# Idle matmuls at the head of a fused attention and feed-forward kernel: 116 tiny ones on four row groups and 11 wide ones, in place of 78 narrow ones

## The chip, the cores and the metric

One core of one Trainium2 chip. The metric is the time of one execution in device microseconds. One early run of the kernel before took 371.03 us and is left out throughout.

## The reference, cut to what matters

```python
# attention inside chunks of 64 tokens: q, k, v are (8, 8, 576, 64)
scores = scale * np.matmul(q_c, k_c.transpose(0, 1, 2, 4, 3))
scores = scores - np.max(scores, axis=-1, keepdims=True)
attn = np.exp(scores)
attn = attn / (np.sum(attn, axis=-1, keepdims=True) + 1e-09)
out = np.matmul(attn, v_c)
# then a feed-forward block on 4608 tokens of 512: w_in is (512, 2048), w_out is (2048, 512)
h = x @ w_in
g = h * (1.0 / (1.0 + np.exp(-beta * h)))
return (g @ w_out)
```

The two big products make up most of the work. The attention of the first tokens has to be done before the first big product can start, so the first 25 us are a chain of small steps.

## The kernel before: the parts that matter here

```python
    def emit_idle(n, w):                       # products of zeros; nobody reads the result
        d = ps_p.tile([128, 512], FP32, tag="p", name="warm")
        for _ in range(n):
            nc.tensor.matmul(out=d[:, 0:w], lhsT=idle[:, 0:128], rhs=idle[:, 0:w])
    ...
        nc.vector.memset(idle, 0.0)
        nc.vector.memset(braw, 0.0)
        ...                                    # loads of q, k, v and the weights are issued here
        emit_idle(78, 128)                     # TensorE has nothing else to do yet
        emit_T_half(0)                         # DVE transposes of the first half of q and k
        emit_sc_half(0, 0)                     # 32 score matmuls: the first group
        emit_ex_half(0, 0)
        emit_idle(4, 512)
        emit_T_half(1)
        emit_sc_half(0, 1)                     # 96 score matmuls in these three: the second group
        emit_ex_half(0, 1)
        emit_sc_half(1, 0)
        emit_sc_half(1, 1)
        emit_ex_half(1, 0, 2)
        ...
        emit_pv(0, ("s", "p"))                 # value matmuls, 32 and 32
        emit_norm(0, 0)                        # DVE: reciprocal and product
        emit_norm(0, 1)
        emit_pv(1, ("x", "p"))
        ...
        emit_xt_pe(0, 0)                       # transposes on TensorE, copies on ACT
        emit_xt_pe(0, 1)
        a0, v0 = emit_m(0, 0, 0, 256, True)    # the first big product starts here
        a1, v1 = emit_m(0, 1, 0, 256, True)
```

Each matmul is two instructions, a weight load and the product (the page of before counts 2754 of each). "Own instruction n" below is the n-th of these in program order.

The softmax here doesn't subtract the row's maximum and nothing guards it: scores larger than these inputs give would overflow.

## Time and profile before

| | before |
|---|---|
| median, lowest of the first runs | 295.28, 294.66 us |
| span of the profiled run | 294.1 us |
| first score group starts | 8.32 us |
| second score group starts | 10.17 us |
| TensorE stops in the value matmuls | 11.62 to 14.94 us |
| first big product starts | 18.40 us |
| half clock | 14.87 to 21.70 us |

Times inside a run count from the span's start. The prediction quotes the lines for most of this. In a timeline line the columns are start, length, engine, source line, operation, tiles, shapes and count, and in brackets the idle time just before and what ended it; "issue" there means that the profile shows nothing that was waited for. PE is a product of TensorE and PEld its weight load; DVE is VectorE, ACT ScalarE and POOL GpSimd. "Half clock" is a granted TensorE clock of 0.5.

### The profile page before, as it was taken

How to read it: one execution, taken by the hardware profiler on the slowest of the kernel's cores; microseconds unless marked ns; L12 is line 12 of the kernel's file. 1: busy time of each engine (PE TensorE's matmuls, PEld its weight loads, DVE VectorE, ACT ScalarE, POOL GpSimd, SP SyncE). 2: the span in 40 equal slices, each digit the busy share in tenths (PEclk: the TensorE clock that was granted, in tenths of full speed). 3: DMA queues.
4: the chain of work that ended last, by engine and by line, in shares of the span. 5: the costliest groups of instructions: out<-in, count | busy, mean ns of one | idle time of the engine just before them, and what ended most of it. 6: DMA issues, size and time to landing. Idle time of an engine off the chain costs nothing.

```text
span 294.1 us, 6595 instructions
## 1 busy us (share of the span) xinstructions
PE 281.8 (96%) x2754; PEld 139.8 (48%) x2754; DVE 140.5 (48%) x250; ACT 147.4 (50%) x225; POOL 95.6 (33%) x124
## 2 busy tenths in 40 slices
PE   8389999999999999999999899999999999999996
PEld 8255445545544444444444444444444444444444
DVE  2367813687455845453545253635363536444300
ACT  4338615785446655445544555545555554544411
POOL 8753768607624796070807060000000000000000
PEclk9959999999999999999999999999999999999999
DMA  8999999999979999999999999242525212101012
GB/s 197 177 197 207 181 175 169 245 108 94 174 98 136 177 178 153 175 159 170 105 187 104 184 116 173 74 107 50 130 72 109 44 63 71 42 36 38 36 71 71
DMA packets 139996, 37.13 MB, mean 126 GB/s; under 512 B 126912, under 2 KB 135488, under 8 KB 139968
## 3 DMA queue, kind: packets, MB, share of 16 engines
q0 software_dynamic: 99136, 17.83, 81.2%
q1 hardware_dynamic: 40688, 18.83, 29.4%
q8 instruction: 21, 0.34, 0.5%
q10 hardware_dynamic: 144, 0.07, 0.1%
q14 instruction: 7, 0.06, 0.1%
HBM read 36.71 MB, written 9.44 MB: 157 GB/s over the span
## 4 chain that ended last, share of the span: by engine, by line
PE 91%; ACT 2%; issue 2%; DVE 2%; DMA 2%; SPq 0%; DVEq 0%
PE hps L310 43%; PE ops L342 41%; PE x L262 2%; DMA raw<-in_k_dram 2%; PE sc L234 1%; PE sc L221 1%; PE ops L543 1%; ACT xt L295 1%; DVE t L175 1%; PE xp L294 1%; DVE x L278 1%; ACT osb L352 0%; ACT h L174 0%; ACT et L204 0%; PE sc L194 0%
## 5 line engine op out<-in xcount | busy, mean ns | idle before, releaser
L324 DVE SCALAR_TENSOR_TENSOR gt<-sg,hps 128x512 f16<-128x512 f32 (+1 forms) x152 | 99.3, 658 | 116.6 <-ACT sg L320 116.4
L310 PE MATMUL hps<-xt,win 128*128 128x512 f16 (+1 forms) x608 | 138.0, 371 | 2.2 <-ACT xt L295 1.2
L320 ACT ACTIVATE sg<-hps,beta 128x512 f32<-128x512 f32 (+1 forms) x152 | 100.4, 665 | 76.0 <-PE hps L310 76.0
L342 PE MATMUL ops<-wout,gt 128*128 128x512 f16 x560 | 131.3, 379 | 0.0
L310 PEld LDWEIGHTS <-win 128*128 128x128 f16 x608 | 58.3, 99 | 64.2 <-issue 3.2
L342 PEld LDWEIGHTS <-gt 128*128 128x128 f16 x560 | 53.7, 98 | 63.1
L352 ACT ACTIVATE osb<-ops 128x512 f32<-128x512 f32 x35 | 20.9, 598 | 42.2 <-PE ops L342 42.2
L110 POOL DMA_DIRECT2D vbig<-in_v_dram x40 | 34.1, 873 | 8.2 <-DMA wout<-in_moe_w_out_dram 3.7
L96 POOL DMA_DIRECT2D qu<-in_q_dram x22 | 18.7, 862 | 45.2 <-DMA qT<-qu 35.2
L278 DVE TENSOR_TENSOR x<-x,rd 128x512 f16<-128x512 f32 x34 | 23.5, 691 | 1.3
L96 POOL DMA_DIRECT2D ku<-in_k_dram x22 | 18.8, 879 | 0.0
L276 DVE RECIPROCAL rd<-x 128x8 f32<-128x8 f32 x34 | 6.8, 201 | 15.4 <-PE x L262 15.4
L262 PE MATMUL x<-vbig,et 64*64 64x65 f16 x544 | 8.1, 196 | 3.5 <-issue 3.3
L262 PEld LDWEIGHTS <-et 64*64 64x64 f16 x576 | 6.4, 111 | 10.1 <-issue 6.4
L243 ACT ACTIVATE et<-sc 128x1024 f16<-128x1024 f32 (+1 forms) x8 | 6.4, 811 | 8.5 <-PE sc L234 8.5
L295 ACT COPY xt<-xp 128x512 f16<-128x512 f16 x12 | 6.7, 588 | 7.6 <-PE xp L294 7.6
L227 ACT ACTIVATE et<-sc 128x1024 f16<-128x1024 f32 x10 | 10.2, 1015 | 0.0
L359 PE MATMUL warm<-idle 128*128 128x128 f16 (+1 forms) x82 | 7.2, 264 | 1.2 <-DVE braw L363 1.2
L102 POOL DMA_DIRECT2D ku<-in_k_dram x9 | 6.8, 752 | 3.4 <-DMA win<-in_moe_w_in_dram 1.5
L102 POOL DMA_DIRECT2D qu<-in_q_dram x9 | 6.8, 761 | 2.5 <-DMA win<-in_moe_w_in_dram 1.3
L359 PEld LDWEIGHTS <-idle 128*128 128x128 f16 x82 | 6.3, 119 | 1.5 <-DVE braw L363 1.2
L555 DVE TENSOR_SCALAR osb<-ops 128x256 f32<-128x256 f32 (+1 forms) x2 | 0.7, 358 | 12.1 <-PE ops L543 12.1
(36 smaller groups left out, 68.8 us busy)
## 6 DMA issues: line engine op xcount, KB each, us to landing
out_dram<-osb SPq DMA_DIRECT2D x35, 256.0 KB, 3.6
vbig<-in_v_dram POOLq DMA_DIRECT2D x32, 128.0 KB, 7.0
qu<-in_q_dram POOLq DMA_DIRECT2D x20, 128.0 KB, 5.0
ku<-in_k_dram POOLq DMA_DIRECT2D x20, 128.0 KB, 6.2
win<-in_moe_w_in_dram POOLq DMA_DIRECT2D x8, 256.0 KB, 9.3
wout<-in_moe_w_out_dram POOLq DMA_DIRECT2D x4, 512.0 KB, 12.1
qu<-in_q_dram POOLq DMA_DIRECT2D x3, 256.0 KB, 7.2
ku<-in_k_dram POOLq DMA_DIRECT2D x3, 256.0 KB, 7.7
```

What stands on the lines that cost most here:

```text
L96: nc.gpsimd.dma_start(out=tv[off:off + n, sp], in_=src[b, :, s:s + n, :].rearrange("h p d -> p h d"),)
L102: nc.gpsimd.dma_start(out=t[off // 2:(off + n) // 2], in_=src[b, :, s:s + n, :].rearrange("h (p r) d -> p h r d", r=2),)
L110: nc.gpsimd.dma_start(out=vbig[off:off + n, i, :, 0:D], in_=v[b, :, s:s + n, :].rearrange("h p d -> p h d"),)
L227: nc.scalar.activation(out=et, in_=sc, func=ACTF.Exp, scale=scale)
L262: nc.tensor.matmul(out=(x[0][64 * c:64 * c + 64, r, g, 0:D + 1] if len(x) == 1 else x[r][64 * c:64 * c + 64, g, 0:D + 1]), lhsT=(et[64 * r ...
L278: nc.vector.tensor_tensor(out=o, in0=z[..., 0:D], in1=rd[:, r].to_broadcast(list(o.shape)), op=ALU.mult)
L310: nc.tensor.matmul(out=hps[:, 0:n], lhsT=w_in16[m // 2][:, kk, (m % 2) * 128:(m % 2) * 128 + 128], rhs=xr[:, c0 // CH:(c0 + n) // CH, 2 * ...
L320: nc.scalar.activation(out=sg[:, 0:n], in_=hps[:, 0:n], func=ACTF.Tanh, scale=beta2[:, m:m + 1])
L324: nc.vector.scalar_tensor_tensor(out=gt_t[j][:, m, c0:c0 + n], in0=sg[:, 0:n], scalar=1.0, in1=hps[:, 0:n], op0=ALU.add, op1=ALU.mult,)
L342: nc.tensor.matmul(out=ops, lhsT=gt_t[j][:, kk, t * 128:(t + 1) * 128], rhs=w_out16[kk // 4][:, kk % 4, :], start=(kk == 0), stop=(kk == K ...
L352: nc.scalar.activation(out=osb, in_=ops, func=ACTF.Copy, scale=0.5)
L359: nc.tensor.matmul(out=d[:, 0:w], lhsT=idle[:, 0:128], rhs=idle[:, 0:w])
```

## The change

The diff doesn't say its intent. In program order it puts 127 idle matmuls, 254 instructions, where 78 with 156 instructions stood, and most of the new ones are very short.

```diff
+    tiny = const.tile([128, 64], FP16)
...
+    def emit_tiny(n):
+        d = [ps_p.tile([128, 512], FP32, tag="p", name="tiny") for _ in range(2)]
+        for i in range(n):
+            c = i % 4
+            p0, o0 = 32 * c, 64 * (c % 2)
+            nc.tensor.matmul(
+                out=d[c // 2][o0:o0 + 64, 0:8],
+                lhsT=tiny[p0:p0 + 32, :],
+                rhs=tiny[p0:p0 + 32, 0:8],
+            )
...
+        nc.vector.memset(tiny, 0.0)
         nc.vector.memset(idle, 0.0)
...
-        emit_idle(78, 128)
+        emit_tiny(116)
+        emit_idle(11, 512)
```

## The prediction

A block in the prediction is what one packet of the instruction queue brings. That the second starts at own instruction 192 and the third at 448 is an estimate from the first profile of before: the stop comes after 447 own instructions, and 5508 own instructions for 21 packets is 262 a packet, taken as 256.

> **What bounds the kernel now.** I read the page first. The span is 294.1 us (timed: 294.66 and 295.45 us; the third run, 371.03 us, is an outlier that I leave out), and the chain that ended last is almost all matmul, so from about 25 us on every microsecond is a matmul of the two big products. A change to idle matmuls at the head can only gain in the first 25 us, and what it gains there must survive to the end. One part of the page points at the place:
>
> ```profile
> PE 91%; ACT 2%; issue 2%; DVE 2%; DMA 2%; SPq 0%; DVEq 0%
> ...
> PEclk9959999999999999999999999999999999999999
> ```
>
> One slice of 40 (14.7 to 22.1 us) has the granted TensorE clock at half, and 2% of the chain (some 6 us) is "issue", time in which an engine waited for nothing that the profile shows. The timeline of TensorE for 7 to 16 us (start, length, what, count, idle time before and its releaser) shows where:
>
> ```profile
> 8.32 0.45 PE L194 MATMUL sc<-t,t 32*64 32x64 f16 x32 [0.97 <-DVE t L175]
> 8.70 1.04 PE L359 MATMUL warm<-idle 128*128 128x512 f16 x4
> 10.17 1.00 PE L194 MATMUL sc<-t,t 32*64 32x64 f16 x96 [0.44 <-DVE bt L397]
> 11.33 0.29 PE L262 MATMUL x<-vbig,et 64*64 64x65 f16 x13 [0.15 <-ACT et L204]
> 14.94 0.27 PE L262 MATMUL x<-vbig,et 64*64 64x65 f16 x3 [3.32 <-issue]
> ```
>
> In the middle of sixteen identical matmuls, after the thirteenth, TensorE stands still for 3.32 us without a releaser. Their operands are the same tiles as those of the thirteen before, so no data is missing. The DMA view of 12 to 13 us shows what came meanwhile, the first packet of this queue in the span:
>
> ```profile
> q8 instruction: 1, 0.02, 5.9%
> ```
>
> I read this as the instruction stream running dry. [...] up to the stop TensorE has run 78 idle matmuls + 32 + 4 + 96 with a weight load each (420 instructions), 13 matmuls and, by the same view for weight loads, 14 weight loads: 447. [...] 21 instruction packets in that queue for 2754 x 2 = 5508 instructions is 262 each, and 0.34 MB / 21 is 16 KB.
>
> The stop costs twice. The windows view (length, busy us and count of PE, PEld, DVE, ACT, POOL, then granted clock, DMA share and GB/s) gives the clock:
>
> ```profile
> 11.50:14.50 3.00, 0.12 (x13) 0.03 (x3) 0.00 (x0) 0.87 (x2) 1.42 (x2) 1.00 1.47 197
> 14.50:15.00 0.50, 0.06 (x5) 0.06 (x8) 0.00 (x0) 0.00 (x0) 0.16 (x1) 0.87 1.46 200
> 15.00:18.00 3.00, 2.20 (x59) 1.44 (x59) 2.58 (x10) 0.82 (x2) 2.06 (x3) 0.50 1.45 196
> 18.00:21.00 3.00, 2.60 (x15) 1.98 (x15) 1.60 (x4) 1.09 (x3) 1.37 (x2) 0.50 1.46 197
> 21.00:22.00 1.00, 1.00 (x10) 0.85 (x9) 0.28 (x1) 0.75 (x3) 0.54 (x1) 0.65 1.46 198
> ```
>
> A mean of 0.87 in the half microsecond from 14.50 puts the drop at 14.87 us, and 0.65 in the microsecond from 21 puts the return at 21.70: 6.8 us at half clock, straight after the idle stretch.
>
> [...] here the 32 matmuls of L194, on several row and column groups, took 0.45 us, less the last one's 0.19 us is 0.26 / 31 = 8.4 ns. The measurement decides: tiny matmuls go at 8 to 14 ns.
>
> **The change, part by part.**
> Removed: 78 idle matmuls of 128 columns (156 instructions), which filled 1.19 to 7.34 us. TensorE then waits to 8.32 us for the transposed q and k, so their end is not on the path.
> Added: a memset of the tiny tile ahead of the others (the 128x32 memset took 0.09 us): the first matmul may start a little earlier, near 1.0 us. Then 116 tiny matmuls: at 8.4 ns (full clock) to 13.6 ns (half clock: the 51 of L262 after 14.94 us took 0.92 us, less 0.24 for the last, over 50), 1.0 to 1.6 us, over at about 2.0 to 2.6 us. Then 11 of 512 columns. At half clock a 256-column one took (1.87 - 0.42) / 7 = 0.21 us (L310 at 18.40), so 0.42 us each; at full clock 0.22 us. All at half: 4.7 us, over by 7.3 us; with a rise on the way, about 6 us. Both are before 8.3 us, so neither delays the attention.
> Moved, and this is the point: the idle stretch now has 127 x 2 = 254 instructions in place of 156, and the first 192 of them [...] are gone by tiny matmul 96, at about 1.0 + 96 x 8.4 to 13.6 ns = 1.8 to 2.3 us. Before, instruction 192 lay in the first 32 score matmuls, near 8.4 us at execution. The fetch of the third block, which I take to be asked for as the second is entered, moves some 6 us forward. Before, boundary to restart took 14.94 - 8.4 = 6.5 us, with the DMA engines full. From 2.3 us that gives 8.8 us. The third block is now needed at own instruction 448, that is 448 - 254 - 72 = 122 instructions into the 192 of the second score group, at about 10.7 us. So it is there, with 2 us to spare, and the 3.32 us stop goes.
>
> What follows, in the order of the chain. The first 16 value matmuls run through from 11.33 us, and the reciprocal starts at 11.9 in place of 15.25 (0.31 us after the sixteenth, as now): 3.35 us earlier. The value tiles landed by then: the last was issued at 5.5 and the median landing is 6.6 us, so 12.1 us, needed at about 12.4. DVE and ACT don't know the clock, so the first big product starts near 18.40 - 3.35 = 15.05 us. Its weights must be there: the queue's wait for the first weight load ended at 14.84 us, so they are, just. With full clock its eight 256-column matmuls take about 1.0 us in place of 1.87; then ACT sets the pace (a copy of 0.58, a tanh of 0.47, a copy of 0.58 us after it, from 16.3 us), and the second half starts at about 18.1 in place of 22.58 us. Sum: 3.35 + 1.1 = 4.4 to 4.5 us.
>
> Given back: block four is asked for at the second boundary, 10.7 us, and by the same 6.3 to 6.5 us comes at about 17.1, where it is needed at own instruction 704 (before's 606, the fourth group of the product), about 17.2 to 17.6: 0 to 0.3 us. The transposes of q and k for the third unit (L154) need a load that lands at 22.60 + 12.0 = 34.6 us; two of 0.7 us make 36.0, and its score matmuls move from 41.68 to 37.2: it holds. The third output weight (landing about 31.6) is needed at 37, the fourth (31.75 + 6.7 = 38.5) at about 42: they hold. From there nothing that the profile shows waits for a load. So about 4.2 us stay: 295.4 - 4.2 = 291.2 us.
>
> **The rivals.**
> First, the clock drops all the same. Even without the stop, TensorE has little to do from 12.5 to 15 us (transposes that wait for DVE), and at 15 to 18 us in the trace 2.2 busy us of 3 didn't raise the clock. Then only the 3.3 us are sure, and some of that goes in slow big matmuls: gain 2.2 to 3.4 us, 292 to 293.2 us. I give it three chances in ten.
> Second, the stop is no fetch, or its fetch isn't tied to the instruction count but to a time. Then it stays, or moves 98 instructions on, into the product, with about the same length: 295 us. The count of 447 speaks against it: one in ten.
> Third, a wait takes its place: weights that land at 14.6 to 24 us at DMA full share, or q and k at 34.6 us. That would cap the gain at 3 to 4 us: 291.5 to 292.5 us. My margins there are from 0.4 to 2 us, so a part of it is likely.
> [...]
>
> **Range and chances.** The main case with a share of the third rival gives 290.7 to 292; the first gives up to 293.2; the second 295. Below 289.5 (2%) would need 5.9 us, more than stop and half clock together are worth on the chain. So 291.2, range 289.9 to 293.8, faster by 2%: 0.06, within: 0.92, slower: 0.02 (a later fetch that stops longer).
>
> **What would show it.** Right: no "issue" gap in the L262 matmuls near 11.6 us; the first packet of the instruction queue before 9 us, in place of 12.5; no half clock between 12 and 22 us; first big product (L311 then) near 15.0 us and the 64-matmul run near 18 us; the same 2754-and-more matmul stream after it, 4 us earlier. Wrong: the gap elsewhere with the same length, half clock in spite of no gap, or a new wait on a weight load.

## The result, and the profile after

Four runs: 291.83 to 292.66 us, median 292.27. The ratio to the kernel before is 0.9903, with a 95% interval of 0.9877 to 0.9928. (A ratio here is the mean time of one kernel's fast runs over that of the other's fast runs of the same rounds, so it isn't quite the ratio of the medians.) A second set on another chip gave 0.9913 (0.9892 to 0.9933). The change is faster by about 0.9%, 2.6 to 2.9 us, and so within 2% of the kernel before. The prediction was 291.2 us with a range of 289.9 to 293.8, and within 2% with a chance of 0.92.

The head of TensorE's timeline in the changed kernel:

```profile
0.96 1.72 PE L367 MATMUL tiny<-tiny 32*64 32x8 f16 x116 [0.96 <-DVE tiny L374]
2.61 4.71 PE L360 MATMUL warm<-idle 128*128 128x512 f16 x11
8.30 0.45 PE L195 MATMUL sc<-t,t 32*64 32x64 f16 x32 [0.98 <-DVE t L176]
8.69 1.04 PE L360 MATMUL warm<-idle 128*128 128x512 f16 x4
10.64 1.37 PE L195 MATMUL sc<-t,t 32*64 32x64 f16 x96 [0.92 <-DVE bt L411]
11.98 0.44 PE L263 MATMUL x<-vbig,et 64*64 64x65 f16 x16
12.18 0.46 PE L263 MATMUL y<-vbig,et 64*64 64x65 f16 x16
...
15.62 1.87 PE L311 MATMUL hps<-xt,win 128*128 128x256 f16 x8 [0.67 <-ACT xt L296]
```

The first sixteen value matmuls run in one piece; the stop of 3.32 us is gone. But the second score group takes 1.37 us in place of 1.00, the eight big matmuls at 15.62 us take 1.87 us as before, so both ran slowly. The DMA view of 5 to 6 us of the changed kernel has its first instruction packet, at 5.37 us by the trace's record, 7 us earlier than before:

```profile
q8 instruction: 1, 0.02, 5.8%
```

The windows view of the changed kernel (stretch, length, busy us and count for PE, PEld, DVE, ACT and POOL, then granted clock, DMA share, GB/s), cut where the clock changed and every 3.41 us between:

```profile
7.03:10.44 3.41, 1.71 (x38) 0.65 (x36) 3.01 (x4) 0.70 (x2) 2.83 (x4) 1.00 1.98 162
10.44:13.85 3.41, 2.73 (x162) 2.46 (x163) 1.49 (x6) 1.73 (x3) 2.97 (x5) 0.50 1.86 180
13.85:17.27 3.42, 2.73 (x16) 1.81 (x15) 2.48 (x10) 1.64 (x3) 1.54 (x3) 0.50 1.45 196
17.27:20.68 3.41, 3.41 (x22) 2.64 (x20) 1.27 (x4) 2.29 (x5) 2.03 (x3) 0.50 1.46 197
20.68:24.09 3.41, 3.41 (x24) 2.15 (x22) 2.32 (x6) 2.63 (x6) 1.50 (x4) 1.00 1.37 203
```

The half clock now starts at 10.44 us, right after a window in which TensorE was busy for 1.71 us of 3.41, and it lasts three such windows, one more than in the first profile of before. Of the ten timed runs of the change, the six with three half-clock windows (mean clock 0.981 or 0.982) average 292.75 us, the four with two (0.987 or 0.988) 291.87 us.

Where the time came from: the first big product starts 2.78 us earlier than in the first profile of before (18.40 to 15.62), and the first matmul of the second big product (34.68 to 32.36) 2.32 us. The spans differ by 3.5 us, because the first profile of before has one more wait that the head doesn't explain. TensorE's timeline of that profile:

```profile
159.58 1.89 PE L342 MATMUL ops<-wout,gt 128*128 128x512 f16 x8
162.50 1.02 PE L310 MATMUL hps<-xt,win 128*128 128x512 f16 x4 [1.03 <-issue]
```

A second profile of the unchanged kernel (experiment 5) doesn't have it, and one of the changed versions (experiment 3) does, at the same place in the program. These four matmuls read `xt`, and in both traces the wait ends 0.09 us after the landing of a transpose through DMA that writes `xt`: 162.41 and 162.50 us, in experiment 3 159.47 and 159.56 us. In the changed kernel that transpose had landed at 156.21 us, before its matmuls at 159.08 us. So a late transpose is the likely cause; why it is late in some executions is not shown. A late instruction packet it is not: between 150 and 162 us the DMA view has one packet of the instruction queue in the first profile of before, at 154.70 us, 7.8 us ahead of the wait's end, and none in experiment 3. Between the second profiles of both kernels (experiments 5 and 6) the start of the second big product differs by 34.82 - 32.46 = 2.4 us, and the spans by 293.1 - 290.7 = 2.4 us: nothing is gained or lost behind the head, and this agrees with the timed 2.6 to 2.9 us.

### The profile page after: what moved, and what is told of

It reads as the page before. It is cut to its first block, busy times and chain, and to the rows that moved or that the text cites.

```text
span 290.6 us, 6694 instructions
## 1 busy us (share of the span) xinstructions
PE 282.9 (97%) x2803; PEld 137.7 (47%) x2803; DVE 140.9 (48%) x251; ACT 147.5 (51%) x225; POOL 95.6 (33%) x124
## 4 chain that ended last, share of the span: by engine, by line
PE 93%; DMA 3%; ACT 2%; issue 1%; POOL 0%; DVE 0%; DVEq 0%; POOLq 0%
PE hps L311 44%; PE ops L343 42%; DMA h<-in_k_dram 3%; PE x L263 2%; PE sc L235 1%; PE sc L222 1%; PE ops L557 1%; PE xp L295 1%; ACT xt L296 1%; PE sc L195 0%; ACT osb L353 0%; ACT et L205 0%; POOL h L380 0%; ACT sg L321 0%; DVE osb L569 0%
## 5 line engine op out<-in xcount | busy, mean ns | idle before, releaser
L321 ACT ACTIVATE sg<-hps,beta 128x512 f32<-128x512 f32 (+1 forms) x152 | 100.4, 665 | 75.3 <-PE hps L311 75.3
L129 POOL DMA_DIRECT2D win<-in_moe_w_in_dram x8 | 6.0, 752 | 1.0 <-DMA h<-in_k_dram 0.6
L176 DVE STREAM_TRANSPOSE t<-h 128x512 f32<-128x512 f32 x4 | 4.3, 1092 | 3.9 <-ACT h L175 3.6
```

The source lines that it names most:

```text
L321: nc.scalar.activation(out=sg[:, 0:n], in_=hps[:, 0:n], func=ACTF.Tanh, scale=beta2[:, m:m + 1])
```

## The experiments

Theory F, an estimate to be tested: TensorE stops because its third block isn't there yet; the block is asked for at own instruction 192 and needed at own instruction 448. The 448 is from the stop after 447 in the first profile of before. The 192 is 256 less, where 256 is an estimate of a block's size: 5508 / 21 = 262 own instructions a packet on that page, and from the first packet to the last TensorE began 240 a packet there (447 to 5250 own instructions over 20 packets) and 250 in the changed kernel (247 to 5505 over 21). Theory C, for the clock, an estimate to be tested too: the granted clock is decided in windows of 3.41 us, by how busy TensorE was. (In the clock records of all the traces, what lies between two changes lasts 3.41, 6.83, 10.24, 13.65, 269.65, 273.07 or 283.31 us: whole multiples of 3.413 us.) Ten kernels ran. The ratios are each to the kernel before; experiments 1 to 4 shared one chip, 5 to 8 another, 9 and 10 the first again.

| | idle matmuls at the head | between the score groups | median us | ratio (95%) | stop, us | first packet at |
|---|---|---|---|---|---|---|
| before | 78 narrow | 4 wide | 295.28 | 1 | 3.32 | 12.48 |
| change | 116 tiny, 11 wide | 4 | 292.27 | 0.9903 (0.9877 to 0.9928) | none | 5.37 |
| 1 | 11 wide, 116 tiny | 4 | 293.76 | 0.9957 (0.9933 to 0.9981) | 0.78 | 10.33 |
| 2 | 11 wide | 4 | 291.55 | 0.9885 (0.9857 to 0.9913) | none | 14.76 |
| 3 | 116 tiny | 4 | 293.05 | 0.9929 (0.9886 to 0.9972) | none | 5.31 |
| 4 | 116 tiny, 13 wide | 7 | 291.34 | 0.9867 (0.9838 to 0.9895) | none | 5.45 |
| 5 | before, again | 4 | 294.87, one run | | 3.08 | 12.37 |
| 6 | change, again | 4 | 292.50 | 0.9913 (0.9892 to 0.9933) | none | 5.55 |
| 7 | 98 tiny, 13 wide | 7, and 2 + 2 later | 290.30 | 0.9848 (0.9827 to 0.9868) | none | 5.51 |
| 8 | none | 4 | 292.33 | 0.9897 (0.9876 to 0.9919) | none | 14.71 |
| 9 | 13 wide | 7, and 2 + 2 later | 293.21 | 0.9934 (0.9917 to 0.9950) | 2.06 | 15.44 |
| 10 | 62 narrow | 4 | 294.24, one run | | 3.09 | 12.61 |

The packet times are the starts of the first packet of the instruction queue in each trace's DMA records. "Stop" is a wait put down to "issue" in the head; experiments 3 and 8 also have one far behind the head (1.2 us at 159.6 us and 0.2 us at 100.4 us), which isn't counted here.

### 1. The same idle matmuls, the wide ones first

```diff
-        emit_tiny(116)
-        emit_idle(11, 512)
+        emit_idle(11, 512)
+        emit_tiny(116)
```

> The same idle matmuls in the other order: 11 wide, then 116 tiny; so the same number of instructions ahead of the work, and the same work. Theory F (the third block's fetch is asked for at the moment when own instruction 192 passes): that moment moves from about 2.3 us to 6.7 to 7.1 us, the first instruction packet from 5.4 to 10 to 11.2 us, and TensorE stops inside the second score group (own instruction 448) until 12.5 to 13.6 us, 2 to 3 us; time 294 to 295 us. Rival R (only where the boundary falls in the work counts, not when it is passed): no stop, 292.3 us.

TensorE's timeline of experiment 1:

```profile
5.42 1.09 PE L367 MATMUL tiny<-tiny 32*64 32x8 f16 x116
8.57 0.64 PE L195 MATMUL sc<-t,t 32*64 32x64 f16 x32 [2.06 <-DVE t L176]
9.15 1.89 PE L360 MATMUL warm<-idle 128*128 128x512 f16 x4
10.96 0.89 PE L195 MATMUL sc<-t,t 32*64 32x64 f16 x60
12.63 0.69 PE L195 MATMUL sc<-t,t 32*64 32x64 f16 x36 [0.78 <-issue]
```

The stop is back, though the number of instructions ahead of it is the same as in the change. It comes after 22 + 232 + 64 + 8 + 120 = 446 own instructions, where theory F puts it, and the packet came at 10.33 us, inside the expected 10 to 11.2 us. So what counts is when the boundary is passed. The rival, that only its place counts, is out. The stop is shorter than the 2 to 3 us expected: the wide matmuls between the score groups ran at half clock (1.89 us for four in place of 1.04), so TensorE came to instruction 446 only at 11.85 us. The time, 293.76 us, is a little below the expected 294 to 295; the stop ended at 12.63 us, at the early end of the expected 12.5 to 13.6 us.

### 2. The wide ones alone

```diff
-        emit_tiny(116)
         emit_idle(11, 512)
```

> Eleven wide idle matmuls alone, 22 instructions. Theory F: own instruction 192 is passed in the second score group at 10.2 to 10.7 us, first instruction packet at 13.2 to 14.8 us, block there at 15.7 to 17.2 us, needed at own instruction 448, which is now at the fourth group of the first big product near 17.3 us: no stop in the value matmuls, at most 0.5 us later; time 292 to 293 us. If an early pass of the boundary is needed for any gain (rival: the tiny ones are what saves it): a stop of 3 us, 295 us.

No stop, as theory F says, and 291.55 us, a little better than expected, though the instruction packet comes at 14.76 us, later than in the kernel before. With 22 instructions at the head in place of 156, own instruction 448 lies behind the eight matmuls of the first big product (15.67 us in this run); it ran at 17.33 us, 2.6 us after the packet's start, and the third block was there. So tiny matmuls aren't needed to remove the stop; fewer instructions do it too.

### 3. The tiny ones alone

```diff
         emit_tiny(116)
-        emit_idle(11, 512)
```

> The 116 tiny ones alone. Theory F: first instruction packet at 5.4 us as with the change, no stop. Clock theory: without wide ones the clock stays at half until about 20 us, which costs some 0.2 us in the first score group only, as the second ran at half with the change too: 292.3 to 292.7 us. Rival (the wide ones carry part of the gain): 293.5 us or more.

The packet is at 5.31 us and there is no stop: theory F holds. The time is inconclusive. The median of 293.05 us lies between both expectations, the four runs spread from 291.82 to 294.13 us, and the profiled one has the wait of 1.2 us near 158 us that the first profile of before had too. The head of the profiled run is no worse than with the change: the second big product starts at 31.41 us, against 32.36. The clock did not do what was expected: it rose at 12.48 us and not near 20 us, fell at 15.89 us and was back at 19.31 us.

### 4. The change with its two gaps partly filled

```diff
-        emit_idle(11, 512)
+        emit_idle(13, 512)
...
-        emit_idle(4, 512)
+        emit_idle(7, 512)
```

> The change with 13 in place of 11 wide ones, and 7 in place of 4 between the two score groups, so that the stretch from 7.0 to 10.4 us has TensorE busy 2.8 in place of 1.7 us. Clock theory (the drop at 10.4 us comes from that half-idle stretch): no drop at 10.4 us, second score group 1.0 in place of 1.37 us, first big product's eight at 1.0 in place of 1.87 us, time 290.8 to 291.6 us. Rival (the drop comes all the same, from the next stretch, or the extra matmuls delay the second score group): 292.3 us or more.

The windows view of experiment 4, from where its clock rose:

```profile
6.10:9.52 3.42, 2.61 (x43) 1.18 (x42) 2.82 (x3) 1.43 (x2) 3.02 (x6) 1.00 1.82 170
9.52:12.93 3.41, 2.14 (x136) 1.47 (x137) 1.75 (x4) 1.69 (x3) 2.78 (x4) 1.00 2.04 171
12.93:16.34 3.41, 2.67 (x45) 1.93 (x46) 3.12 (x11) 1.18 (x3) 2.12 (x4) 0.50 1.45 198
```

Half right. With 2.61 us busy the clock stays, and the second score group takes 1.00 us, as expected. But the next window, with 2.14 us, loses it at 12.93 us, so the first eight big matmuls still take 1.87 us. The median of 291.34 us is inside the expected 290.8 to 291.6 us. One of the four runs lists a mean clock of 1.0, so no half clock came after its clock's first rise, and it is the fastest: 290.30 us, against 291.33 to 291.76 us of the three with one or two half-clock windows. It is a single run.

### 5 and 6. Both kernels again, for a second profile

> The kernel before, unchanged, for a second profile. If its stop is the fetch of a block: the gap is at the same instruction (after the thirteenth value matmul), with the first instruction packet some 2.5 us ahead of its end. The 1.03 us wait at 161 us in its first profile: if it belongs to the kernel, it is here too; if chance, it need not be. If the landing of the second half of k at 9.5 us (8.7 us in the first profile of before) comes from the run and not from the early fetch, it may be 9.5 us here too.

> The change, unchanged, on the chip of the next two: ratio 0.990 to the kernel before, no stop near 11.6 us, first instruction packet near 5.4 us; three half-clock windows in some executions and two in others, as in its first four.

The stop of before is at the same matmul, and 3.08 us long. TensorE's timeline of experiment 5:

```profile
11.30 0.29 PE L262 MATMUL x<-vbig,et 64*64 64x65 f16 x13 [0.15 <-ACT et L204]
14.67 0.26 PE L262 MATMUL x<-vbig,et 64*64 64x65 f16 x3 [3.08 <-issue]
```

The wait near 161 us isn't there, so it isn't a constant of the kernel. The clock in this run dropped at 12.83 us and was back at 23.07 us: three windows, where the first profile of before had two. The kernel before changes between both states too, without a clear difference in its times. The second half of k lands at 8.7 us again (2.12 + 6.6), against 2.12 + 7.4 = 9.5 us in the change. Experiment 6 repeats the change: 0.9913, no stop, the packet at 5.55 us.

### 7. More filling: two wide ones after the first value matmuls, two ahead of the first big product

```diff
-        emit_tiny(116)
-        emit_idle(11, 512)
+        emit_tiny(98)
+        emit_idle(13, 512)
...
-        emit_idle(4, 512)
+        emit_idle(7, 512)
...
         emit_pv(0, ("s", "p"))
+        emit_idle(2, 512)
...
         emit_xt_pe(0, 1)
+        emit_idle(2, 512)
         a0, v0 = emit_m(0, 0, 0, 256, True)
```

> The filled version of the fourth experiment (13 wide at the head, 7 between the score groups) with two more wide ones after the first value matmuls and two ahead of the first big product, and 98 in place of 116 tiny ones (the boundary at instruction 192 is still passed by a tiny one). Clock theory: fewer or no half-clock windows after 12.9 us, first big product at 15.2 to 15.4 us with its eight at 1.0 us, 290.0 to 291.0 us, and below the change by 1.2 to 2 us. Rival (the stretch waits for DVE and ACT anyhow, or the added matmuls stand in the way of the first big product): equal to the fourth experiment, 291.3 us, or worse.

The windows view of experiment 7 from where its clock rose, and then TensorE's timeline of the first big product:

```profile
6.29:9.70 3.41, 2.52 (x43) 1.16 (x42) 2.66 (x4) 1.30 (x2) 2.83 (x6) 1.00 1.87 168
9.70:13.12 3.42, 2.69 (x153) 1.65 (x155) 1.83 (x4) 1.69 (x3) 2.91 (x4) 1.00 1.98 174
13.12:16.53 3.41, 2.76 (x55) 1.88 (x44) 3.00 (x11) 1.63 (x3) 2.11 (x4) 1.00 1.45 197
```

```profile
15.37 1.03 PE L311 MATMUL hps<-xt,win 128*128 128x256 f16 x8 [0.24 <-ACT xt L296]
```

The clock never drops, the first big product starts at 15.37 us and its eight matmuls take 1.03 us. 290.30 us, the best of all: 1.5% below the kernel before, and 0.9848 / 0.9913 = 0.993 of the change. The rival, that the stretch waits for DVE and ACT anyhow, is out: the second big product starts at 30.26 us, against 32.46 us in the profile of the change (experiment 6) and 31.81 us in experiment 4. The times don't show that this version beats experiment 4: the intervals of the two ratios overlap (0.9827 to 0.9868 and 0.9838 to 0.9895), and they are from two chips.

### 8. No idle matmuls at the head

```diff
-        emit_tiny(116)
-        emit_idle(11, 512)
```

> No idle matmul at the head at all (four between the score groups stay). Theory F: own instruction 192 is passed in the second score group at 11 us, first instruction packet near 14.5 us, own instruction 448 only needed after the third group of the first big product, near 18.5 us: no stop. Clock theory: clock at half until 12 us or more, as with tiny ones alone. Time 291.8 to 293 us, so better than before: the 78 idle matmuls of before cost more by their number than they gain by warmth. Rival (idle matmuls are worth their place): 295 us or more.

0.9897 against 0.9913 for the change, with overlapping intervals: no idle matmuls are as good as the change. The 78 narrow ones of before cost 3 us. There is no stop, and the clock's record starts only with the rise at 21.31 us: what was timed until then ran at half (the first score group took 0.64 us in place of 0.45, the four wide ones between the score groups 1.89 us in place of 1.04, the first eight big matmuls 1.87 us in place of 1.03). The mean clock that this run lists, 1.0, is therefore wrong for the head: what lies before this trace's first clock record was counted as full.

### 9. Experiment 7 without its tiny ones

```diff
-        emit_tiny(98)
         emit_idle(13, 512)
```

> The filled version of the seventh experiment without its 98 tiny ones. Theory F: own instruction 192 is now passed in the second score group, about 11 us, the first instruction packet comes at 14.5 to 15 us and the block is there 2.3 to 2.5 us after, at 16.9 to 17.4 us. Own instruction 448 is 26 + 64 + 14 + 192 + 64 + 4 + 64 + 16 + 4 = 448: the first matmul of the first big product, ready at about 15.4 us. So a stop of 1.5 to 2 us just there, and 291.3 to 292.3 us, 1.3 us or more above the seventh. Rival (the tiny ones have no part in it, only the wide ones that keep the clock): no stop, 290.3 us.

TensorE's timeline of experiment 9:

```profile
8.63 3.08 PE L360 MATMUL warm<-idle 128*128 128x512 f16 x7
11.65 1.00 PE L195 MATMUL sc<-t,t 32*64 32x64 f16 x96
...
15.38 0.38 PE L360 MATMUL warm<-idle 128*128 128x512 f16 x1
17.81 0.39 PE L360 MATMUL warm<-idle 128*128 128x512 f16 x1 [2.06 <-issue]
18.04 1.62 PE L311 MATMUL hps<-xt,win 128*128 128x256 f16 x8
```

The stop is back, in the place computed ahead to within one matmul: after 446 own instructions, and 2.06 us long (expected 1.5 to 2). So once the filling has added instructions, the tiny ones earn their place: they bring the fetch forward (first packet at 5.51 us in experiment 7, at 15.44 us here). The time, 293.21 us, is above the expected 291.3 to 292.3 us. The seven wide ones between the score groups ran at half clock in this run, 3.08 us, and held the second score group up until 11.65 us (10.80 us in experiment 7), which I hadn't counted. So the stop is not all of what this version loses to experiment 7.

### 10. The kernel before with 62 narrow ones

```diff
-        emit_idle(78, 128)
+        emit_idle(62, 128)
```

> The kernel before with 62 in place of 78 narrow idle matmuls, 32 instructions fewer. Theory F: the stop stays at own instruction 448, which is now 124 + 64 + 8 + 192 = 388 and 60 more: after the thirtieth value matmul in place of the thirteenth or so, and ends near 14.7 us as before (the boundary at 192 is still passed at the score matmuls). The first reciprocal no longer waits for it: near 11.9 us in place of 15.2. Rival (the stop belongs to the first value matmuls, a wait on data that the profile doesn't show): the gap stays after the thirteenth.

TensorE's timeline of experiment 10:

```profile
11.41 0.32 PE L262 MATMUL x<-vbig,et 64*64 64x65 f16 x16 [0.15 <-ACT et L204]
11.54 0.29 PE L262 MATMUL y<-vbig,et 64*64 64x65 f16 x13
14.92 0.27 PE L262 MATMUL y<-vbig,et 64*64 64x65 f16 x3 [3.09 <-issue]
```

The stop has moved by sixteen matmuls, exactly the number taken out, from after the thirteenth to after the twenty-ninth value matmul (I had expected the thirtieth), and it ends at the same time. It belongs to a place in the instruction stream and not to a wait on data. The first reciprocal runs at 11.78 us (expected 11.9).

## Why the prediction was right, and where it wasn't

**The stop is an instruction fetch: right, and shown.** In the two profiles of before and in experiments 1, 9 and 10 it comes after 446 or 447 own instructions, in four different places of the program: after the thirteenth and after the twenty-ninth value matmul, after the sixtieth score matmul of the second group, and after an idle matmul. Each time it ends 2.3 to 2.5 us after the packet starts (12.48 to 14.94, 12.37 to 14.67, 10.33 to 12.63, 15.44 to 17.81, 12.61 to 14.92 us). That the trigger is own instruction 192 is supported by experiment 1 against the change (the same stream, the packet at 10.33 or 5.37 us as the tiny ones come late or early), and by all twelve traces: own instruction 192 runs at 2.2 to 12.0 us, and the packet starts 3.1 to 4.2 us after it each time. A few instructions more or fewer would fit as well.

**The tiny ones, 1.0 to 1.6 us: right in size.** They took 1.72 us, less 0.19 us for the last: 13.3 ns each, at the slow end of 8 to 14 ns; in experiment 1, at full clock, they took (1.09 - 0.19) / 115 = 7.8 ns each. (The estimate had left out the length of the last one.) The wide ones ran at half clock to the end, over at 7.3 us, as the worst case of the working had it.

**The third block in time: right.** Estimated at 8.8 us, needed at 10.7 us; the packet came at 5.37 us, so with the 2.3 to 2.5 us of the other runs it was there, by estimate, at about 7.8 us.

**The step that failed: "with full clock its eight 256-column matmuls take about 1.0 us in place of 1.87".** They took 1.87 us. (DVE and ACT kept their pace, as predicted: in the changed kernel ACT's 128x512 copy took 0.59 us at 14.36 us, at half clock, and at 51.12 us, at full, and DVE's 128x512 product 0.69 us at 12.71 and at 43.30 us.) I looked for a drop of the clock only between 12.5 and 15 us. It came at 10.44 us, from the window of 7.03 to 10.44 us, whose gaps at 7.3 and 9.7 us I had called harmless because nothing waited in them. Of the 4.4 us that I had on the way to the second half of the first big product (predicted at 18.1 us, in the trace at 19.87 us), some 0.6 us were lost by the start at 15.62 in place of 15.05 us and 1.2 us on half clock after that, and another 0.4 us as the half clock lasted to 20.68 us; 2.3 us stayed. The first rival, "the clock drops all the same", with 292 to 293.2 us, is what happened, and I had given it three chances in ten. The time lies in the range because the range took in this rival; the main figure of 291.2 us was 1.1 us too low. Experiment 7, which keeps the clock, shows that the size was real: its second big product starts 34.68 - 30.26 = 4.4 us earlier than in the first profile of before, and its time is 290.3 us, 0.9 us beyond my main case.

**A part of the 0.6 us isn't explained.** The second score group started 0.47 us later than before, because the second half of k landed at 9.5 us and not at 8.7 us (the load's issue at 2.12 us plus its time to landing in the DMA view, 7.4 and 6.6 us). A landing of 9.4 to 9.6 us was seen in the change twice and in experiments 2, 3, 4 and 7, of 8.6 to 8.7 us in both profiles of before and in experiment 8, and 9.1 to 9.3 us in 1, 9 and 10. The early instruction packet can't be its cause, as experiment 2 has none; what is stays open. The group then took another 0.37 us at half clock, part of which overlapped with ACT.

**The rival of weights that come late** took nothing that can be seen: TensorE waits for no load in the changed kernel's head. The fourth block cost nothing, where 0 to 0.3 us had been set aside: its packet came at 14.86 us and own instruction 704 (448 + 256, by the same estimate) ran at 18.98 us.

**Theory C.** In the windows that I cut, at full clock, those with TensorE busy for 0.16 to 2.14 us of 3.41 were followed by half clock (before 0.16, change 1.71, experiments 1, 2, 3, 4 and 5: 1.78, 1.10, 1.89, 2.14 and 1.60), and those with 2.52 us or more were not (before 2.55, experiment 4 2.61, experiment 5 3.11, experiment 7 2.52, 2.69 and 2.76). At half clock 2.26, 2.67, 2.73 and 2.99 us didn't bring it back, and 3.30, 3.40 and 3.41 us did. The other traces, cut at their own edges, agree but for one window, of experiment 10:

```profile
5.62:9.04 3.42, 2.07 (x57) 1.67 (x55) 3.03 (x3) 1.35 (x3) 3.34 (x6) 1.00 1.68 176
9.04:12.45 3.41, 2.06 (x128) 1.41 (x127) 1.82 (x5) 2.02 (x4) 2.90 (x5) 1.00 2.17 167
```

The clock stayed after the first of these and fell after the second, with the same busy time. So near 2 us the busy time that the profile shows doesn't decide alone; what else does is not shown. These are the profile's modelled busy times and a few windows of each trace; the edge of a window falls elsewhere in every execution, and experiments 4 and 7 are the only ones that changed the filling on purpose. That busier windows kept the clock in these traces is shown, but for the one above; a threshold is not.

## What to carry to other kernels

The idle matmuls here also used up instructions of the stream: with 78 narrow ones, 156 own instructions, the stop of 3.32 us fell into the value matmuls, and with none at the head (experiment 8) there was no stop. At a stop without a releaser, count the own instructions ahead of it (446 or 447 in five traces here) and look for a packet of the instruction queue inside it (here it started 2.3 to 2.5 us ahead of the stop's end). Then either take instructions away (experiments 2 and 8) or put the cheapest ones first, so that the packet comes early (the change, 5.37 us). For the clock, look at whole windows (3.41 us here): a gap in which nothing waited still cost the clock for the next one to four windows (experiments 3 and 9 had one, experiments 1 and 2 four), and filling such gaps (experiment 7) made some two fifths of the gain of the best version, (0.9913 - 0.9848) / (1 - 0.9848). Test the removal of a warm-up first: without any idle matmul at the head this kernel was as fast as with the change.
